# One v block turned on TensorE, next-batch loads reordered, and idle products around the first softmax

## The chip, the cores and the metric

One Trainium2 chip, one of its cores. The time is device microseconds of that core, median of several executions; lower is better. The engines are TensorE (PE), its weight loads (PEld), VectorE (DVE), ScalarE (ACT), GpSimd (POOL) and SyncE (SP). SP and POOL issue most of the DMAs.

## The reference, cut to what matters

```python
B, N, C = 4, 6080, 256          # q, k, v: [B, N, C] float32
qn = q / (norm(q, axis=1) + 1e-6);  kn = k / (norm(k, axis=1) + 1e-6)
a  = softmax(kn.T @ qn / tau)   # per batch, 256 x 256
x  = (v @ a).reshape(B * N, C)
out = gelu_tanh(x @ w_in) @ w_out        # w_in [256, 2048], w_out [2048, 256]
```

The kernel folds `a` into the first weight matrix (`aw = a @ w_in`, once a batch). A block of 512 rows of v then needs: v turned (channels on the partitions, `vT`), products of the hidden layer (`hp`), gelu by ACT, products with `w_out` (`yp`). The Gram matrix `G` and the column sums of the next batch are spread as "slots" between the steps of the blocks; for batch 0 they form a first phase of their own.

## The kernel before: the parts concerned

Loads of v and of the later q and k are issued by POOL and cast from f32 to bf16 on the way; turning v is a DMA transpose issued by SP. `b` counts batches, `nb` blocks.

```python
    vin = ctx.enter_context(tc.tile_pool(name="vin", bufs=5))
    ...
    first_chunks = chunks_of([2, 5, 6, 6, 6, 6, 6, 4, 3, 2, 1], 7)   # the 64-row remainder goes with chunk 7
    TAIL = 7
    ...
    def pairs_of(n, sqb):                       # column sums of a chunk's squares, for n < TAIL
        size = first_chunks[n][1]
        h = size // 2
        ...                                     # slots 0..size-1 only
    ...
    def turn_v(nb):
        ...
        for s in range(n):
            nc.sync.dma_start_transpose(out=vT[:, :, s * 128 : s * 128 + 128], in_=t[:, s, :])
    ...
    # POOL's queue: w_in (4 loads), v block 1, w_out (2 loads), then
    for n in range(3):
        load_qk(1, n)                           # chunks of the next batch
        if n < 2:
            load_v(n + 2)
    ...                                         # softmax of batch 0, vT of block 0 by PE
        nc.scalar.activation(vT0[:, cc, :], vps[:, cc, :], AF.Copy)   # in two halves
    ...
    turn_v(1)                                   # then in the block loop: turn_v(nb + 2); load_v(nb + 4)
```

## Time and profile before

| stretch of the kernel before (us) | what runs | PE busy |
|---|---|---|
| 0 to 36.9 | loads of q and k of batch 0, G, column sums | 60%, from 29.5 on 87% |
| 36.9 to 46.3 | softmax, aw, vT of block 0 | 76% |
| 46.3 to 54.5 | block 0 | 97% |
| 54.5 to 64.6 | nothing on PE | 0% |
| 64.6 to 81.7 | block 1 | 98%, at first at half clock |
| 81.7 to 775.2 | blocks 2 to 47 | 99% |

776.3 us (775.14 to 776.45, four executions). Read from the right: once block 2 has begun, PE works without a break, so the time is the start of block 2 plus a constant. Everything the change can win must show as an earlier block 2.

### The profile page before, as it was taken

How to read it: one execution, taken by the hardware profiler on the slowest of the kernel's cores; microseconds unless marked ns; L12 is line 12 of the kernel's file. 1: busy time of each engine (PE TensorE's matmuls, PEld its weight loads, DVE VectorE, ACT ScalarE, POOL GpSimd, SP SyncE). 2: the span in 40 equal slices, each digit the busy share in tenths (PEclk: the TensorE clock that was granted, in tenths of full speed). 3: DMA queues.
4: the chain of work that ended last, by engine and by line, in shares of the span. 5: the costliest groups of instructions: out<-in, count | busy, mean ns of one | idle time of the engine just before them, and what ended most of it. 6: DMA issues, size and time to landing. Idle time of an engine off the chain costs nothing.

```text
span 775.2 us, 12214 instructions
## 1 busy us (share of the span) xinstructions
PE 739.3 (95%) x5155; PEld 507.8 (66%) x5240; DVE 277.9 (36%) x487; ACT 420.9 (54%) x413; POOL 65.2 (8%) x121
## 2 busy tenths in 40 slices
PE   4776999999999999999999999999999999999998
PEld 3534666666666666666667666666766666666666
DVE  4731454544521454544431264545351101110011
ACT  5752555555555555555545555555545555555552
POOL 0231011001210001000300010100100000000000
PEclk9987999999999999999999999999999999999999
DMA  9999568412983365721695167723432333212111
GB/s 367 319 193 174 105 127 144 82 41 63 187 140 82 76 126 99 149 52 41 119 173 112 38 130 133 132 55 78 85 69 80 67 69 89 60 50 74 40 55 52
DMA packets 82039, 83.86 MB, mean 108 GB/s; under 512 B 56640, under 2 KB 61504, under 8 KB 81984
## 3 DMA queue, kind: packets, MB, share of 16 engines
q0 software_dynamic: 17648, 32.97, 25.8%
q1 hardware_dynamic: 64048, 49.18, 23.7%
q8 instruction: 41, 0.67, 0.4%
q10 hardware_dynamic: 288, 0.92, 0.3%
q14 instruction: 14, 0.11, 0.0%
HBM read 78.91 MB, written 24.90 MB: 134 GB/s over the span
## 4 chain that ended last, share of the span: by engine, by line
PE 90%; DMA 6%; SPq 1%; issue 1%; ACT 1%; POOL 0%; DVE 0%; ACTq 0%; DVEq 0%
PE yp L432 44%; PE hp L484 41%; PE G L124 4%; DMA st<-in_k_dram 3%; DMA vT<-vb 2%; DMA vb<-in_v_dram 1%; PE ps L184 1%; SPq L276 0%; POOL win_bf L291 0%; ACT sqb L230 0%; SPq L78 0%; PE cols L136 0%; ACT g L488 0%; PE T L162 0%; DVE qkb L225 0%
## 5 line engine op out<-in xcount | busy, mean ns | idle before, releaser
L488 ACT ACTIVATE g<-hp 128x1024 bf16<-128x1024 f32 (+1 forms) x384 | 389.6, 1015 | 327.1 <-PE hp L484 307.6
L484 PE MATMUL hp<-vT,aw 128*128 128x512 bf16 (+1 forms) x1458 | 385.4, 378 | 14.0 <-DMA vT<-vb 10.1
L432 PE MATMUL yp<-wout_bf,g 128*128 128x256 bf16 (+1 forms) x3072 | 397.9, 273 | 0.8 <-issue 0.2
L432 PEld LDWEIGHTS <-g 128*128 128x128 bf16 (+1 forms) x3072 | 301.1, 98 | 114.7 <-issue 3.3
L484 PEld LDWEIGHTS <-aw 128*128 128x128 bf16 x1536 | 149.8, 98 | 117.9 <-issue 14.5
L449 DVE COPY ysb<-yp 128x512 f32<-128x512 f32 (+1 forms) x93 | 64.0, 689 | 402.7 <-PE yp L432 402.7
L373 DVE TENSOR_TENSOR acc<-acc,sq 128x512 f32<-128x512 f32 (+1 forms) x141 | 97.5, 692 | 4.8
L124 PE MATMUL G<-qkb 128*128 128x256 bf16 (+1 forms) x384 | 74.0, 296 | 14.9 <-DVE qkb L225 14.9
L372 DVE TENSOR_TENSOR sq<-qkb 128x512 bf16<-128x512 bf16 (+1 forms) x141 | 58.7, 417 | 0.0
L124 PEld LDWEIGHTS <-qkb 128*128 128x128 bf16 (+1 forms) x384 | 39.0, 105 | 23.4 <-DVE qkb L225 15.8
L262 POOL DMA_DIRECT2D vb<-in_v_dram x47 | 25.5, 543 | 213.0 <-DMA vT<-vb 204.7
L193 DVE TENSOR_SCALAR aw<-ps,rsinv 128x512 bf16<-128x512 f32 x30 | 22.4, 749 | 26.2 <-PE ps L184 21.2
L78 POOL DMA_DIRECT2D qkb<-in_q_dram x24 | 13.2, 549 | 203.0 <-PE G L124 119.3
L230 ACT ACTIVATE sqb<-st 128x3072 bf16<-128x3072 f32 (+5 forms) x10 | 21.1, 2123 | 10.6 <-DMA st<-in_k_dram 10.6
L225 DVE CAST qkb<-st 128x3072 bf16<-128x3072 f32 (+6 forms) x12 | 14.6, 1225 | 15.0 <-DMA st<-in_k_dram 15.0
L184 PE MATMUL ps<-win_bf,eT 128*128 128x512 bf16 x54 | 17.1, 394 | 0.1
L383 POOL TENSOR_TENSOR r<-r,half 128x4 f32<-128x4 f32 x3 | 3.1, 1038 | 142.1 <-DVE r L382 142.1
L78 POOL DMA_DIRECT2D qkb<-in_k_dram x24 | 13.2, 549 | 4.5 <-DMA wout_bf<-in_moe_w_out_dram 1.9
L408 DVE RECIPROCAL den<-den 128x256 f32<-128x256 f32 x6 | 10.5, 1753 | 0.2
L453 DVE COPY ysb<-yp 64x256 f32<-64x256 f32 (+1 forms) x7 | 2.7, 415 | 21.2 <-PE yp L432 21.2
L184 PEld LDWEIGHTS <-eT 128*128 128x128 bf16 x60 | 5.9, 101 | 2.5 <-issue 1.1
L212 DVE TENSOR_TENSOR pair<-sqb 128x1536 bf16<-128x1536 bf16 (+2 forms) x7 | 5.8, 836 | 0.0
(51 smaller groups left out, 66.5 us busy)
## 6 DMA issues: line engine op xcount, KB each, us to landing
out_dram<-ysb SPq DMA_DIRECT2D x44, 512.0 KB, 2.9
vb<-in_v_dram POOLq DMA_DIRECT2D x43, 256.0 KB, 5.6
qkb<-in_q_dram POOLq DMA_DIRECT2D x21, 384.0 KB, 6.0
qkb<-in_k_dram POOLq DMA_DIRECT2D x21, 384.0 KB, 8.0
st<-in_q_dram SPq DMA_DIRECT2D x5, 768.0 KB, 10.4
st<-in_k_dram SPq DMA_DIRECT2D x5, 768.0 KB, 12.1
vT<-vb SPq DMA_TRANSPOSE x188, 3.8
out_dram<-ysb SPq DMA_DIRECT2D x4, 384.0 KB, 2.4
```

Of the source, the lines that this page charges most:

```text
L78: engines[x].dma_start(out=dst[:, x, 0:size, :], in_=src[b, s0 * 128 : (s0 + size) * 128, :].rearrange("(p s) c -> p s c", s=size))
L124: nc.tensor.matmul(G[:, ic, :], lhsT=qk[:rows, 1, s, ic * 128 : ic * 128 + 128], rhs=qk[:rows, 0, s, :], start=first and ic == 0, stop=las ...
L184: nc.tensor.matmul(ps, lhsT=eT[:, jc, ic * 128 : ic * 128 + 128], rhs=win_bf[:, jc, fs * 512 : fs * 512 + 512], start=jc == 0, stop=jc == 1)
L193: nc.vector.tensor_scalar_mul(dst, ps, scale)
L230: nc.scalar.activation(sqb[:rows, :, lo:hi], st[:rows, :, lo:hi], AF.Square)
L262: nc.gpsimd.dma_start(out=t[:, 0:n, :], in_=v_rows[r0 : r0 + n * 128, :].rearrange("(p s) c -> p s c", s=n))
L372: nc.vector.tensor_mul(sq[:rows], flat, flat)
L373: nc.vector.tensor_add(acc[:rows], acc[:rows], sq[:rows])
L432: nc.tensor.matmul(yp[:rows, at, :], lhsT=g[:, fc, s * 128 : s * 128 + rows], rhs=wout_bf[:, fc, :], start=fc == 0, stop=fc == FC - 1)
L449: nc.vector.tensor_copy(ysb[:, s0 : s + 1, :], yp[:, 0 : s + 1 - s0, :])
L484: nc.tensor.matmul(hp[:, j, :cols], lhsT=aw[:, cc, fc * 128 : fc * 128 + 128], rhs=vT[:, cc, :cols], start=cc == 0, stop=cc == 1)
L488: nc.scalar.activation(g[:, 2 * i : 2 * i + 2, :cols], hp[:, :, :cols], AF.Gelu_apprx_tanh)
```

## The change

Its intent: take away the 10 us wait for block 1's turned v, and keep PE's clock up through the softmax. Core of the diff:

```diff
-    vin = ... bufs=5          # and in the loop: load_v(nb + 4)
+    vin = ... bufs=4          #                  load_v(nb + 3)
-    first_chunks = chunks_of([2, 5, 6, 6, 6, 6, 6, 4, 3, 2, 1], 7)
+    first_chunks = chunks_of([2, 5, 6, 6, 6, 6, 6, 4, 3, 2, 1], 1)
+            # chunks 9 and 10 are loaded into the unused slots of the tiles of chunks 7 and 8
+                st = staged[n - 2][:, :, first_chunks[n - 2][1] :, :]
+    def keep_clock(n):
+        for _ in range(n):
+            idle = pH.tile([128, 2, 512], FP32, tag="h", name="idle")
+            nc.tensor.matmul(idle[:, 0, :], lhsT=filler[:, 0:128], rhs=filler, start=True, stop=True)
+        if n >= TAIL - 2:
+            keep_clock(size)             # before G of chunks 5 to 10; also 5 and 1 in the softmax
-    for n in range(3):
-        load_qk(1, n)
-        if n < 2:
-            load_v(n + 2)
+    load_qk(1, 0)
+    load_v(2)
-        nc.scalar.activation(vT0[:, cc, :], vps[:, cc, :], AF.Copy)
+    nc.scalar.activation(vT0, vps, AF.Copy)
-    turn_v(1)
+    def turn_v_on_pe(nb): ...            # 8 PE transposes of bf16, one DVE copy
-        if b > 1:
-            for n in range(3):
-                load_qk(b, n)
-        for _ in range(10):
+        for n in range(10):
+            if n % 3 == 0 and n < 9 and (b, n // 3) not in loaded_of:
+                load_qk(b, n // 3)
+            if b == 1 and n == 5:
+                turn_v_on_pe(1)
             yield
```

More of the change, by code (lines that the diff above doesn't have):

```diff
@@ L54 @@
     gp = ctx.enter_context(tc.tile_pool(name="gp", bufs=2))
-    vin = ctx.enter_context(tc.tile_pool(name="vin", bufs=5))
+    vin = ctx.enter_context(tc.tile_pool(name="vin", bufs=4))
     pA = ctx.enter_context(tc.tile_pool(name="pA", bufs=2, space=bass.MemoryType.PSUM))
@@ L89 @@
     n_all = S_ALL + 1
-    first_chunks = chunks_of([2, 5, 6, 6, 6, 6, 6, 4, 3, 2, 1], 7)
-    TAIL = 7
+    first_chunks = chunks_of([2, 5, 6, 6, 6, 6, 6, 4, 3, 2, 1], 1)
+    TAIL, SHARED = 7, 9
     staged = []
@@ L97, in stage_chunk @@
         if n < len(first_chunks):
-            st = stage.tile([128, 2, SMAX, 256], FP32, tag="st", name="st")
+            if n < SHARED:
+                st = stage.tile([128, 2, SMAX, 256], FP32, tag="st", name="st")
+            else:
+                st = staged[n - 2][:, :, first_chunks[n - 2][1] :, :]
             load_chunk((nc.sync, nc.scalar if n < 2 else nc.sync), st, 0, first_chunks[n])
@@ L106 @@
     make_identity(nc, ident)
+    ident_bf = const.tile([128, 128], BF16)
+    nc.gpsimd.tensor_copy(ident_bf, ident)
+    filler = const.tile([128, 512], BF16)
+    nc.gpsimd.memset(filler, 1.0)
     ones_bf = const.tile([128, 1], BF16)
@@ L307 @@
     Gs = scaled(G, r)
+    keep_clock(5)
     T = turned(Gs)
@@ L318 @@
                              rhs=ident, is_transpose=True)
-        nc.scalar.activation(vT0[:, cc, :], vps[:, cc, :], AF.Copy)
+    nc.scalar.activation(vT0, vps, AF.Copy)
+    keep_clock(1)
     nc.scalar.activation(dummy, ones_f, AF.Gelu_apprx_tanh)
@@ L348, with turn_v_on_pe @@
     vT_of[0] = vT0
-    turn_v(1)
-    def attention_steps(b, aw_next):
-        if b > 1:
-            for n in range(3):
-                load_qk(b, n)
-        for _ in range(10):
+    def turn_v_on_pe(nb):
+        t = v_of.pop(nb)
+        vT = vts.tile([128, 2, 512], BF16, tag="vT", name="vT")
+        p = pA.tile([128, 2, 512], BF16, tag="a", name="vps")
+        for cc in range(2):
+            for s in range(4):
+                nc.tensor.matmul(p[:, cc, s * 128 : s * 128 + 128],
+                                 lhsT=t[:, s, cc * 128 : cc * 128 + 128],
+                                 rhs=ident_bf, is_transpose=True)
+        nc.vector.tensor_copy(vT, p)
+        vT_of[nb] = vT
+    def attention_steps(b, aw_next):
+        for n in range(10):
[3 more added lines that the diff above has]
+                turn_v_on_pe(1)
             yield
@@ L472 @@
             turn_v(nb + 2)
-            load_v(nb + 4)
+            load_v(nb + 3)
             g = gp.tile([128, FC, 512], BF16, tag="g", name="g")
```

## The prediction

> **What bounds the kernel now.** I read the page first. TensorE (PE) is busy 739.3 of 775.2 us and the chain that ended last is 90% PE, so from about 70 us on only PE work counts. The windows view says so by stretch: 528.65 of 532.00 us busy from 113 to 645. What can be had lies in the first 82 us. Page lines:
>
> ```profile
> PE   4776999999999999999999999999999999999998
> PEclk9987999999999999999999999999999999999999
> L484 PE MATMUL hp<-vT,aw 128*128 128x512 bf16 (+1 forms) x1458 | 385.4, 378 | 14.0 <-DMA vT<-vb 10.1
> L432 PE MATMUL yp<-wout_bf,g 128*128 128x256 bf16 (+1 forms) x3072 | 397.9, 273 | 0.8 <-issue 0.2
> vT<-vb SPq DMA_TRANSPOSE x188, 3.8
> ```
>
> Of the 14.0 us that PE idled before a product of the hidden layer (hp), one wait is 10.1 us: it waits for turned v (vT). A DMA transpose of v lands after 3.8 us in the median. The chain of waits over 28 to 130 us says what stands before it:
>
> ```profile
> 33.50 3.53 POOL win_bf L291 x4
> 37.03 9.48 DMA vb<-in_v_dram
> ...
> 50.44 14.06 DMA vT<-vb
> 64.63 1.44 PE hp L484 x3
> ```
>
> Block 1 of v landed at 46.51, its four transposes were issued from 46.53 to 50.44, and the last landed at 64.49, 14.06 us after its issue and almost four times the median. The windows view (us, then busy time of PE, weight load, DVE, ACT, POOL, the granted clock, DMA share, GB/s) gives the stretches: block 0, the wait, the start of block 1, its rest, block 2:
>
> ```profile
> 46.30:54.50 8.20, 7.95 (x37) 3.32 (x34) 3.28 (x5) 6.87 (x7) 1.43 (x3) 1.00 1.29 197
> 54.50:64.60 10.10, 0.04 (x1) 0.00 (x1) 0.69 (x1) 1.10 (x2) 3.33 (x7) 0.71 1.12 204
> 64.60:70.20 5.60, 5.35 (x23) 3.06 (x25) 0.00 (x0) 1.67 (x2) 0.53 (x1) 0.61 1.12 206
> 70.20:81.70 11.50, 11.45 (x83) 8.01 (x83) 3.77 (x7) 6.35 (x7) 0.00 (x0) 1.00 1.04 94
> 81.70:97.40 15.70, 15.59 (x111) 10.66 (x112) 8.59 (x17) 8.26 (x9) 1.59 (x3) 1.00 0.57 118
> ```
>
> The reader is to see three things: 10.1 us with no PE work; then 5.6 us at a mean clock of 0.61; and DMA engines full (share over 1) until about 75. The DMA view over 50 to 64 us tells who fills them:
>
> ```profile
> q0 software_dynamic: 1251, 2.53, 97.9%
> q1 hardware_dynamic: 1151, 0.26, 16.1%
> ```
>
> Queue q0 carries the casting loads (v, next q and k), q1 at that time only the transposes. They get nearly one packet each, 1251 to 1151, but a transpose's packet is a tenth the size. The transposes are slow because they take turns with a queue that is never empty.
>
> **What the Trainium skill says.** "DMA: Bandwidth & Descriptors", section "Queues, rings and completion order": each DMA engine goes round robin between the queues with work, a packet at a time. The counts above agree. "Advanced Engine Details and Errata", section "X-Bar Transpose (TRN2)", says transposes are as fast as regular DMAs; here they moved 0.26 MB in 14 us beside a full queue, so I use the measurement. "TensorE: Matmul & The Clock Gate", Part 1: after an idle window of about 3.4 us the clock drops to half, and returns after a busy window. The trace agrees: half speed from 58.8 to 69.0 us by the clock's records, three such windows, and also 38.3 to 45.1. Part 4 of that page gives about 275 to 390 ns for one PE transpose; the f32 ones here show 421 ns each at half clock, pipelined.
>
> **The change, part by part.**
>
> Block 1 turned on PE. Removes four DMA transposes and the 10.08 us wait. Adds eight bf16 transposes, which at 128 columns against 512 are about a quarter of an hp product (0.216 us warm): with their loads 0.5 to 0.8 us, and one VectorE copy of about 1 us. They stand between the sixth and seventh step of block 0, where ACT (1.02 us per gelu against 0.86 us of PE) sets the pace, so I count 0.5 us. Data are in time: vb of block 1 landed at 46.5, this place comes near 50. Without the idle stretch block 1 starts warm. From 64.63 to 81.74 it took 17.1 us; warm it takes 8 x (0.86 + 0.87) us plus some five pairs of G products at 0.22, about 15.0. Gain 2.1.
>
> Idle products: 22 before the six last chunks plus six in the softmax stretch, 512 columns each. In the first chunks of these PE may still be cold (0.43 us each, 2.6 us for six), but it has about 0.7 us idle per 3.77 us chunk and turns warm there; the loads, not PE, bound this phase (420 GB/s). In the tail (4+3+2+1, 2.2 us warm) they fill nearly all of PE's slack, about neutral together with the earlier last loads. In 38.3 to 45.1 they may keep the clock up: eight vps transposes, four first aw products at 0.22 instead of 0.42, and one ACT copy instead of two with a handshake. win_bf caps it (its second quarter landed near 42.4). First gelu about 44.2 instead of 46.35: gain 2.1.
>
> Shared stage tiles, remainder moved to chunk 1: the last chunks' loads need no tile release (they waited until 25.6 and 30.5), which removes a dip of the DMA rate (131 GB/s in the one microsecond from 33 to 34) of some 0.5 us; the v0 load also goes earlier. The gate that starts the casting loads moves little, 0.3 us. A side effect, seen in the instruction order: four column-sum products vanish, because the pair sums of chunk 1 do not include its 64-row remainder. Batch 0's norms then miss 64 of 6080 rows, about 0.5% of a norm; scores are tiny, so I expect it to pass, but it is a defect.
>
> Load order: v blocks 2 and 3 now go out before the second chunk of the next batch. Nothing makes POOL wait for PE's slots; only the order in its queue changes. Block 2's own place, behind win, v1, wout and the first chunk, is the same.
>
> **Where block 2 comes in.** Adding up, PE would be ready for block 2 at 44.2 + 8.2 + 0.5 + 15.0 = 67.9 instead of 81.74: a gain of 13.8. But block 2 needs its own four DMA transposes. In the kernel before, its vb landed at 60.55 (SP resumed transposing at 60.57) and the fourth transpose, issued at 64.36, took 14.1 us: 78.4, only 3.3 us ahead of its use. The change moves this landing as follows.
> - vb of block 2: gate 0.3 earlier, and no transposes beside the loads from 46.5 to 60.5. q0 moved 0.80 MB per 4 us in 42 to 50 but 2.53 MB per 14 us in 50 to 64 (0.20 against 0.18 MB/us): 1.2 earlier. So about 59.0.
> - q0 then still has v3, two chunks, v4 and a third chunk: 256 + 768 + 768 + 256 + 768 KB = 2.88 MB, at 0.181 MB/us 15.9 us: empty near 75. (v5 reuses v2's buffer, so it waits for these transposes.)
> - Four transposes at some 300 packets, against q0's turn rate of about 78 packets per us: 15.4 us plus some 2 of latency, 76.4; but they finish at once when q0 empties, as the before trace shows (q0's last landing 78.09, transpose 78.44).
>
> So vT of block 2 lands near **75.0**, and PE idles some 7 us at 67.9: the same wait, one block later. It also drops the clock again; the restart at 64.63 was cold for 4.4 us and lost 2.1; I take 2.4. All gains of head, block 1 and idle products go into this wait, because the end follows the landing. From block 2 on the program is the same length: 776.3 - (81.74 - 75.0) + 2.4 = **772.0 us**.
>
> **The rivals.**
> (1) No new wait: all 13.8 us stay, 762.5. For it: v3 no longer sits behind two chunks, and the author plainly wants the loads spread. Against it: v2's place is unchanged and POOL runs ahead, so q0 stays full. 10%.
> (2) New wait and longer: if vb of block 2 is not earlier at all, and the transposes take the full 18 us that block 1's took (46.53 to 64.49), vT lands at 78 and cold costs 3.4: 776, no gain. 15%.
> (3) PE becomes the bound of the first phase through cold idle products (2.6 us each in two chunks) and delays the first gelu. Then the wait at block 2 shrinks by as much, and the total hardly moves. This is why I do not spread the range for the head.
> (4) Fewer v buffers (4 for 5) give a later wait: v loads still lead their transposing by a block (15.6 us) against landings of 4 to 9 us. Under 5%.
>
> **Range and chances.** Landing 73.5 to 77 and a cold cost of 1.7 to 3.4 give 770 to 775; with rival 1 as a tail below, 767 to 775. Faster by over 2% needs 15.5 us, more than even rival 1 gives: 0.03. Slower by over 2%: 0.01. Within 2%: 0.96.
>
> **What would show it.** PE's wait for vT before hp near 65 gone, but one of 4 to 9 us before block 2's first hp, ending at 73 to 77; granted clock at half around it; block 1 at 15 us and full clock; first gelu near 44; q0 full until 75; PE busy time up by about 6 us of idle products. A landing of block 2's vT before 69 would make me wrong downward, by up to 10 us.

## The result

768.84 us (767.55 to 769.48) against 776.32: ratio 0.9905, 95% interval 0.9888 to 0.9922. All ratios here are the mean time of one kernel's fast runs over that of the other's fast runs of the same rounds, so they are not quite the ratio of the quoted medians. The forecast of 772.0 (767 to 775, "within 2%") held, but only by the tail that I had added for rival 1: the path that I thought likely gave 770 to 775. The gain was 7.5 us where I had 4.3.

The groups of the page that answer to those shown of before (line, engine, what, then busy us, mean ns, idle us before it and what ended it):

```profile
L460 PE MATMUL yp<-wout_bf,g 128*128 128x256 bf16 (+1 forms) x3072 | 397.9, 273 | 0.0
L512 PE MATMUL hp<-vT,aw 128*128 128x512 bf16 (+1 forms) x1536 | 391.8, 378 | 4.3 <-DMA vT<-vb 4.0
...
vT<-vb SPq DMA_TRANSPOSE x184, 3.8
```

The 10.1 us wait is gone and a wait of 4.0 us for vT stands in its place. The stretches of the changed kernel (columns as in the prediction): block 0, block 1, the new wait, the half-clock stretch, the rest of block 2:

```profile
44.10:53.90 9.80, 9.45 (x50) 4.35 (x49) 4.60 (x7) 7.97 (x8) 2.48 (x5) 1.00 1.29 197
53.90:68.10 14.20, 14.20 (x103) 9.87 (x101) 4.58 (x9) 8.16 (x8) 2.65 (x5) 1.00 1.11 211
68.10:72.20 4.10, 0.07 (x1) 0.03 (x1) 3.97 (x8) 0.04 (x1) 0.00 (x0) 0.76 1.36 152
72.20:77.10 4.90, 4.90 (x17) 2.02 (x18) 0.69 (x1) 1.02 (x1) 1.02 (x2) 0.50 0.96 210
77.10:90.10 13.00, 13.00 (x95) 9.17 (x94) 3.77 (x7) 7.02 (x7) 1.09 (x3) 1.00 0.46 82
```

Block 1 now runs at full clock from end to end. PE is done with it at 68.2, stands for 4.0 us, and then works 4.9 us at a clock of 0.50. The chain of waits says what it stood for:

```profile
45.48 11.08 DMA vb<-in_v_dram
56.58 1.29 SPq L292
57.93 2.08 SPq L292
60.07 1.24 SPq L292
61.35 10.72 DMA vT<-vb
72.20 1.86 PE hp L512 x4
```

This is the chain of the kernel before, one block later: v of block 2 lands at 56.56, SP issues four transposes, the last takes 10.7 us. The DMA view of 56.6 to 71.3 us shows the same company (queue, packets, MB, share of the engines):

```profile
q0 software_dynamic: 960, 2.46, 85.6%
q1 hardware_dynamic: 1475, 0.34, 28.8%
```

Start of block 2: 81.74 before, 72.20 now, 9.54 earlier. Block 2 lasts longer by the half clock: before it ran from 81.74 to 97.37 (15.6 us), now from 72.20 to 90.12 (17.9 us), 2.3 lost. Net 7.2 of the 7.5 us between the two profiled spans (775.2 and 767.7).

### The profile page after: what moved, and what is told of

It reads as the page before. It is cut to its first block, busy times and chain, and to the rows that moved or that the text cites. A ratio compares the mean times of both kernels' runs of the same rounds, so it can differ in the third digit from the quotient of the medians.

```text
span 767.7 us, 12360 instructions
## 1 busy us (share of the span) xinstructions
PE 746.8 (97%) x5272; PEld 508.3 (66%) x5272; DVE 278.6 (36%) x488; ACT 420.6 (55%) x412; POOL 65.9 (9%) x123
## 4 chain that ended last, share of the span: by engine, by line
PE 90%; issue 4%; DMA 4%; SPq 1%; POOL 1%; DVE 0%; POOLq 0%
PE yp L460 43%; PE hp L512 41%; PE G L138 4%; DMA vb<-in_v_dram 1%; DMA vT<-vb 1%; PE ps L198 1%; DMA win_bf<-in_moe_w_in_dram 1%; SPq L292 1%; POOL win_bf L307 0%; PE cols L150 0%; PE T L176 0%; POOL filler L114 0%; DVE ysb L481 0%; POOL ident masks.py:199 0%; POOL ident_bf L112 0%
## 5 line engine op out<-in xcount | busy, mean ns | idle before, releaser
L512 PE MATMUL hp<-vT,aw 128*128 128x512 bf16 (+1 forms) x1536 | 391.8, 378 | 4.3 <-DMA vT<-vb 4.0
L78 POOL DMA_DIRECT2D qkb<-in_q_dram x24 | 13.2, 551 | 186.1 <-PE G L138 102.1
L244 ACT ACTIVATE sqb<-st 128x3072 bf16<-128x3072 f32 (+5 forms) x10 | 21.0, 2120 | 10.1 <-DMA st<-in_k_dram 10.1
L239 DVE CAST qkb<-st 128x3072 bf16<-128x3072 f32 (+6 forms) x12 | 14.6, 1225 | 15.2 <-DMA st<-in_k_dram 15.2
L78 POOL DMA_DIRECT2D qkb<-in_k_dram x24 | 13.3, 553 | 2.7 <-DMA wout_bf<-in_moe_w_out_dram 1.9
L134 PE MATMUL idle<-filler 128*128 128x512 bf16 x28 | 7.9, 401 | 0.0
(58 smaller groups left out, 73.5 us busy)
```

The source lines that it names most:

```text
L78: engines[x].dma_start(out=dst[:, x, 0:size, :], in_=src[b, s0 * 128 : (s0 + size) * 128, :].rearrange("(p s) c -> p s c", s=size))
L244: nc.scalar.activation(sqb[:rows, :, lo:hi], st[:rows, :, lo:hi], AF.Square)
L512: nc.tensor.matmul(hp[:, j, :cols], lhsT=aw[:, cc, fc * 128 : fc * 128 + 128], rhs=vT[:, cc, :cols], start=cc == 0, stop=cc == 1)
```

## The experiments

Each time is the median of four to six executions, with those of the kernel before in the same rounds; the three groups of four kernels ran on three chips, on which the kernel before took 777.1, 776.85 and 776.58 us. All outputs passed the comparison with the reference.

The theory: **the end follows the landing of block 2's DMA transposes, these are slow only because the casting queue beside them never empties, and what the other parts save before that is swallowed by the wait.** The rivals: each part saves its own; or the transposes are slow by themselves.

### e1: the PE turn alone

```diff
 # the kernel before, plus:
+            if b == 1 and n == 5:
+                turn_v_on_pe(1)
```

> The kernel before with block 1 of v turned on the PE and nothing else of the change. Theory (the end follows the landing of block 2's DMA transposes, and the other parts of the change feed a wait): vb of block 2 lands near 56.6 us as in the changed kernel, then 3072 KB stand in the casting queue at about 0.2 MB/us, so vT of block 2 lands near 72.6; PE arrives near 70 and waits 1 to 4 us; total 767 to 769.5, the same as the changed kernel's 768.8 within 1.5 us. Rival (each part saves its own): turning alone removes 10.1 us wait and 2.1 us cold clock but the head's 2 us are missing, so it would be 2 us or more slower than the changed kernel, 771 or above.

Measured 770.86 us (767.98 to 772.29), ratio 0.9917 (0.9900 to 0.9934). The changed kernel's own second measurement gave 0.9893 (0.9879 to 0.9906) on another chip. So the turn alone brings most of the gain, but my number missed by more than 1 us and the intervals nearly part: not as clean as the theory wanted. The profiled execution (the fastest, 767.98) shows no wait before block 2 at all, though vT of block 2 landed where I expected it (72.88 for 72.6): the head came late, with the first gelu at 49.36 instead of 46.35 and PE still at half speed, so PE was ready for block 2 only at 73.02. (The head is what runs before block 0: first phase, softmax and first products with `aw`.) This was the first sign that the head varies from run to run.

### e2: the changed kernel without idle products

```diff
-        for _ in range(n):
+        for _ in range(0):
             idle = ...
```

> The changed kernel with its 28 idle products taken out. Theory: whatever they gain before block 2 goes into the 4.0 us wait for vT of block 2, so the total stays within 1.5 us of 768.8 (767 to 770); the first gelu comes about 1.5 to 2 us later, the wait shrinks by as much, and if it falls below some 3 us the clock may not drop, which would even save up to 2 us. Rival (idle products earn their head gain): 770.5 to 772.

Measured 768.39 us, ratio 0.9892 (0.9875 to 0.9908): no loss. First gelu at 46.79 instead of 44.32, and the wait for vT shrank from 4.0 to 1.6 us. Idle products do bring the head forward here, and the wait takes all of it, as the theory said:

```profile
PE hp L512 <- DMA vT<-vb: 1.6, 1, 1.6
```

After this shorter wait the clock did not drop (it stayed at full from 45.56 us to the end of the work), as the expectation allowed for; that profiled execution took 767.02 us, 2.5 less than that of the changed kernel (769.48).

### e3: block 2 turned on PE as well

```diff
+                if b == 1 and seen == 3:
+                    turn_v_on_pe(2)
-            turn_v(nb + 2)
+            if nb > 0:
+                turn_v(nb + 2)
```

> The changed kernel with block 2 of v turned on the PE as well, in block 1. Theory: the 4.0 us wait and the 2.2 us of half clock after it go, eight PE transposes cost 0.4: 768.8 - 4.0 - 2.2 + 0.4 = 763.0, range 762 to 764.5; the transposes of block 3 land by about 72, long before their use at 84. Rival (the wait only moves one block on once more): a new wait of 3 us or more before block 3, 766 to 769.

Measured 763.74 us (763.60 to 764.06), ratio 0.9832 (0.9819 to 0.9846). No wait for vT is left in the list of waits, and the clock stays at full from 25 us to the end. Block 3's four transposes land at 71.9 as expected, long before their use at 84. They were slow as well, 15.2 us from the first issue at 56.74, but block 3 is far enough away, so the wait did not move on again.

### e4: POOL held until block 2's transposes are done

```diff
+            if b == 1 and n == 3:       # POOL reads the four pieces of vT before it goes on to load
+                nc.gpsimd.tensor_copy(gate[:, 1:5], vT_of[2][0:1, 0, ::128])
             if n % 3 == 0 and n < 9 and (b, n // 3) not in loaded_of:
                 load_qk(b, n // 3)
```

> The changed kernel, but POOL waits for the four transposes of block 2 before it issues the second chunk's loads, so the casting queue runs empty while they go. Theory (the transposes are slow only because they take turns with the casting queue): they land within 5 to 7 us of vb of block 2, near 62 instead of 72; no wait before block 2, full clock; 768.8 - 6.2 = 762.6, range 761.5 to 765, unless the held chunk is then late for its G products at block 2. Rival (transposes are slow by themselves, 15 us for four): landing stays near 70, total 767 to 770 or worse.

Measured 763.04 us (762.99 to 764.71), ratio 0.9828 (0.9813 to 0.9843). This is the deciding run. The DMA view of 56.6 to 62.5 us, once the casting queue is empty:

```profile
q1 hardware_dynamic: 1152, 0.26, 22.9%
q0 software_dynamic: 3, 0.00, 0.4%
...
vT<-vb SPq DMA_TRANSPOSE x5, 2.4
```

The same transposes now land 2.4 us after issue, in the median, instead of 8.7 to 11.6 for those of block 2 in the changed kernel. The four of block 2 were issued from 56.09 and all had landed at 62.53: 6.4 us instead of the 15.5 (56.58 to 72.06) in the changed kernel. The windows show block 1 and block 2 back to back at full clock:

```profile
53.10:68.10 15.00, 15.00 (x107) 10.39 (x107) 4.57 (x9) 8.94 (x9) 4.77 (x9) 1.00 0.58 101
68.10:83.80 15.70, 15.70 (x112) 10.62 (x111) 8.62 (x17) 8.23 (x9) 1.60 (x3) 1.00 1.09 212
```

The held loads (DMA share 1.09 in the second line) cost PE nothing. The rival "slow by themselves" is out. Shown is that the queued loads make them slow; whether by the turns alone or also by the time that the loads take from the engines, this run doesn't separate.

### e5: block 2's v loaded ahead of the next batch's first chunk

```diff
-    load_qk(1, 0)
-    load_v(2)
+    load_v(2)
+    load_qk(1, 0)
```

> The changed kernel with vb of block 2 loaded ahead of the next batch's first chunk, the same loads in all. Its vb should land near 53 instead of 56.6 us. Theory (the four transposes take 15 to 19 us beside a full casting queue, and end at the latest when that queue empties near 71): vT of block 2 lands between 69 and 72, so most of the wait stays and the total is within 2 us of the changed kernel, 767 to 769.5. Rival (landing follows the start of the transposes one to one, 15.5 us as measured): 68.6, wait below 1 us, no drop of the clock, 763 to 765.

Measured 769.23 us, ratio 0.9906 (0.9892 to 0.9919), the changed kernel beside it on the same chip 768.62. The list of waits:

```profile
PE hp L512 <- DMA vT<-vb: 4.2, 1, 4.2
```

v of block 2 did land 4 us earlier (52.49 for 56.56), but its fourth transpose landed at 72.35 for 72.06, and the last casting load before it at 71.99. Starting earlier was worth nothing here: the four transposes took 19.8 us instead of 15.5, and the last landed when the casting queue emptied. This reordering, with the same loads in the queue, doesn't cure the wait; other orders were not tried.

### The changed kernel again

> The changed kernel once more, on the same chip as the three runs beside it. Every theory: 768 to 770, half clock after the wait in most runs, ratio to the kernel before 0.989 to 0.992.

768.62 us, ratio 0.9893 (0.9879 to 0.9906). Its profiled execution took 767.58, the other profiled one 769.48. Of the 1.9 us, 1.1 come from an earlier landing of block 2's vT (70.95 here, 72.06 there), and 0.8 from the clock: it stayed at half until 74.20 here and until 77.09 there, and block 2 took 17.1 and 17.9 us.

### e6 and e7: variants of e3

e6 is e3 without idle products (edit as in e2); e7 is e3 with the remainder's squares put back:

```diff
         if size % 2:
             parts.append(sqb[:, :, size - 1, :])
+        if first_chunks[n][2]:
+            parts.append(sqb[:REM, :, size, :])
```

> Blocks 1 and 2 turned on the PE as in e3_turn_two, without the 28 idle products. Theory (idle products bring the first gelu from about 46.8 to 44.1 us, and this counts once no wait behind it swallows it): 2 to 4 us slower than e3_turn_two, 766 to 768, and with a wider spread from run to run. Rival (idle products are worth nothing, as taking them out of the changed kernel suggests): within 0.5 us of 763.7.

> e3_turn_two with the 64-row remainder of chunk 1 put back into the first batch's column sums (four products of one column more). Every theory: within 0.7 us of e3_turn_two, 763 to 764.5; correct, with the norms of batch 0 complete.

e6: 763.85 us (763.45 to 764.18), ratio 0.9832, the same as e3. My theory of 2 to 4 us is refuted for this kernel: without idle products, in all five executions, nothing was lost. In the profiled one the clock was at half from 31.5 to 38.4, under the last chunks, and at full through the softmax; the first gelu came at 44.32. Up to there e6 and e2 run the same instructions, yet e2's profiled execution (on another chip) had half clock from 42.14 to 45.55 and its first gelu at 46.79.

e7: 764.01 us, within 0.3 of e3. The defect that I had read from the instruction order (the pair sums of chunk 1 leave out its 64 rows) is mended at no cost that these runs can tell. The changed kernel passes without it, but its norms of batch 0 are incomplete.

### e8 to e11: what the small parts are worth once the wait is gone

All on one chip. e8 is e4 with the mended sums. e9 is e4 with unshared stage tiles and the remainder back in chunk 7. e10 is e4 without idle products and with vT of block 0 copied in two halves. e11 is the kernel before with only the PE turn, the load order of the change and the hold of e4:

```diff
 # e9, from e4
-    first_chunks = chunks_of([2, 5, 6, 6, 6, 6, 6, 4, 3, 2, 1], 1)
-    TAIL, SHARED = 7, 9
+    first_chunks = chunks_of([2, 5, 6, 6, 6, 6, 6, 4, 3, 2, 1], 7)
+    TAIL, SHARED = 7, 99
 # e10, from e4 (and keep_clock over range(0), as in e2)
-    nc.scalar.activation(vT0, vps, AF.Copy)
+        nc.scalar.activation(vT0[:, cc, :], vps[:, cc, :], AF.Copy)
 # e11, from the kernel before (with the edit of e1 and the slots' loads and gate copy of e4)
-    for n in range(3):
-        load_qk(1, n)
-        if n < 2:
-            load_v(n + 2)
+    load_qk(1, 0)
+    load_v(2)
+    load_v(3)
```

> e4_held with the 64-row remainder of chunk 1 back in the first batch's column sums: the version meant to beat both kernels and to be complete. Every theory: within 0.7 us of e4_held, 762.5 to 764, full clock, no wait before block 2.

> e4_held with the stage tiles not shared and the remainder back in chunk 7, as in the kernel before. Theory (the last loads landed at 35.3 us in the changed kernel as in the one before, so the earlier issues gained nothing): within 0.7 us of e4_held. Rival (the earlier last loads bring 1 us or more that nothing behind swallows here): 764.5 or above.

> e4_held without idle products and with block 0's turned v copied by ACT in two halves, as before. Theory after e6 (idle products worth nothing): what remains of the head's 2 us is this copy, so 0.5 to 2 us over e4_held, 763.5 to 765.5. Rival (the head's gain was the clock after all, by luck granted in e6): 765 to 767 with a spread of over 2 us between runs.

> The kernel before with only two edits: block 1 turned on the PE, and the second chunk's loads behind block 2's transposes (POOL waits for them). Theory: these two hold nearly the whole gain, first gelu near 46, block 2 right after block 1 near 70 to 71: 763.5 to 766.5, below the changed kernel's 768.7. Rival (the small parts of the change, added up, are worth 4 us or more once no wait swallows them): 767 or above.

| kernel | us | range | ratio | first gelu in the profile |
|---|---|---|---|---|
| e8 | 763.28 | 763.11 to 763.66 | 0.9832 (0.9818 to 0.9846) | 44.36 |
| e9 | 763.19 | 762.83 to 764.45 | 0.9835 (0.9820 to 0.9850) | 44.04 |
| e10 | 766.34 | 765.05 to 767.71 | 0.9871 (0.9852 to 0.9889) | 48.55 |
| e11 | 767.89 | 765.37 to 768.26 | 0.9880 (0.9862 to 0.9899) | 49.88 |

e8 is the version to keep: 13.3 us under the kernel before, 5 to 6 under the changed one, and complete (so is e9, where the remainder is in chunk 7 again). e9 confirms that sharing the stage tiles is worth nothing: in the changed kernel the last chunk landed at 35.33, in the one before at 35.32.

e10 and e11 show what e2 hid. With the wait gone, an old head costs 3.1 us (e10 against e8) and 4.6 (e11 against e8). So the rivals of e10 (765 to 767, spread over 2 us) and of e11 (767 or above) were right with their numbers, and my theories were not: the small parts of the head do count, once nothing behind them swallows their gain. Both kernels fall into two groups, though: e10 two executions at 765.05 and 765.53 and two at 767.16 and 767.71, e11 two at 765.37 and 765.85 and three from 767.89 to 768.26. Both profiles are of the slow kind, and a median depends on how many of each were drawn. The PE timeline of e10's head (start, busy, what), and under it the changed kernel's:

```profile
36.16 1.44 PE L138 MATMUL G<-qkb 128*128 128x256 bf16 x6
...
41.85 1.06 PE L331 MATMUL vps<-ident,v 128*128 128x128 f32 x4
43.60 1.11 PE L331 MATMUL vps<-ident,v 128*128 128x128 f32 x4 [0.69 <-ACT vT L334]
...
44.66 1.87 PE L343 MATMUL ps<-win_bf,eT 128*128 128x512 bf16 x4
```

```profile
35.33 0.82 PE L138 MATMUL G<-qkb 128*128 128x256 bf16 x6
...
40.16 1.04 PE L331 MATMUL vps<-ident,v 128*128 128x128 f32 x8
...
41.36 1.02 PE L343 MATMUL ps<-win_bf,eT 128*128 128x512 bf16 x4
```

The same products take nearly twice as long in e10: there PE did not reach full speed before 46.92 us, and in e11 not before 49.56. In eight profiled executions with idle products the first gelu came between 44.00 and 44.36; in the six without (before, e1, e2, e6, e10, e11) between 44.32 and 49.88. In these profiles the idle products buy a head that does not vary.

What stays open: e10 lost both the idle products and the single copy, e6 only the idle products and lost nothing. That the single copy alone always keeps the clock up is ruled out by e2, which has e6's head and came late in its profile; why e6 was early in all five executions, these runs do not tell. e11's further 1.5 us over e10 stand mostly in the head in the two profiles (first gelu 1.3 us later), and the faster groups of the two are only some 0.3 us apart; whether the stage tiles or the v buffers, in which they differ too, have a part in it was not tested.

## Why the prediction was right

**What bounds, and where the gain ends: right.** The 10.1 us wait went, and the wait for block 2's vT that I put in its place came, for the reason given; e3 and e4 remove it in two different ways and are 5.1 us (763.74) and 5.8 us (763.04) below the changed kernel's 768.84, though on another chip.

**PE's arrival at block 2: 67.9 predicted, 68.2 measured.** Its parts held as well: first gelu 44.2 against 44.32, block 1 15.0 us against 15.1 (53.02 to 68.17). But the gain of 2.1 in the head was counted from the one profile of the kernel before (46.35); with the same head e1 and e11 show 49.36 and 49.88.

**The landing of vT: the mis-sized term.** I had v of block 2 at 59.0 and vT at 75.0; measured 56.56 and 72.06, outside the 73.5 to 77 from which I had made my range. The step that failed is "1.2 earlier" for loads that no longer run beside transposes. I took it from the rate of bytes moved (0.20 against 0.18 MB/us). What counts is landings. Between the landing of v block 1 and v block 2 lie the same 1984 KB in both kernels: 14.04 us before (46.51 to 60.55), 10.04 us now (46.52 to 56.56). So without the transposes the loads gained 4.0 us, not 1.2. e1, whose only edit is the PE turn, has 10.09 (45.61 to 55.70), so it is the missing transposes and not another part of the change. (The gate gave 0 instead of 0.3: the first casting load went out at 33.45 before and 33.47 now.) The profile before held the warning: from 46.6 to 60.5 its casting queue moved 2.53 MB while 2.03 MB landed; in the changed kernel, from 46.6 to 56.5, it moved 2.04 MB for the same 2.03. Why moving and landing come apart beside transposes is not shown. The rest of the sum held: 2816 KB after it took 14.7 us (56.56 to 71.30) where I had 15.9, and vT landed 0.8 us after the queue's last load.

**The cold clock: 2.4 predicted, 2.3 measured**, though the wait was 4.0 and not 7 us. That it fits so well is luck: in the other two profiles with such a wait block 2 lost 1.5 (the changed kernel again) and 1.6 us (e5).

**The sum.** (81.74 - 72.06) - 2.3 = 7.4, beside 7.5 measured; I had (81.74 - 75.0) - 2.4 = 4.3.

**Parts that I had wrong but which the wait made harmless.** The square root that ends the first phase began at 38.07 instead of 36.95. That is not the cost of the idle products alone: without them it began at 38.82 in e2 and 38.34 in e6, and with the head of the kernel before at 39.15 in e1 and 39.59 in e11. The profile of the kernel before had the clock at full from 28.04 to 38.28; e2 and e6 had it at half under the last chunks, e1 and e11 all through. The shared tiles gained nothing instead of 0.5 us. Rival 3 said why a later head would not show: the wait shrinks by as much. e2 shows the exchange, 4.0 to 1.6 us.

**Rivals.** Rival 1 (no new wait, 762.5) is what e3 and e4 reach when its condition is made true: 763.7 and 763.0. Rival 2, a longer wait, did not come. Rival 4, the fewer v buffers, left no trace: the list of waits holds no other wait for vT.

**The page of the skill behind the clock.** "TensorE: Matmul & The Clock Gate", Part 1, gave the drop after an idle window; the changed kernel shows it again, 0.50 from 70.27 to 77.09 around a 4.0 us wait. The moment differs from the page's window of about 3.4 us: here the drop came 2.1 us after PE's work had ended at 68.17, and in e5 only at 73.31, when PE had started again at 72.49. After the wait of 3.1 us in the changed kernel's second profile it dropped too, after e2's of 1.6 us it did not.

## What to carry to other kernels

When a wait is removed, look at once for the next consumer of the same kind of transfer, and compute when its data land, not only when the engine will be ready; all gains upstream of that landing are worth nothing until it moves. Small transfers beside a queue that stays full are slow: here four transposes took 15.5 to 19.8 us, or 6.4 once the queue was held. Holding the other queue (e4) helped, starting the small one earlier (e5) did not. And judge small changes again after a wait behind them is gone: what measured as nothing in e2 belonged to a head worth 3 to 5 us in the medians of e10 and e11.

## What the Trainium skill lacked or had wrong

- "Advanced Engine Details and Errata", "X-Bar Transpose (TRN2)": transposes as fast as regular DMAs. Here, on free engines (e4), their packets took 22.9% of 5.9 us for 0.26 MB, by my estimate 5 us of all 16 engines a MB, as the casting loads did in the changed kernel (85.6% of 14.7 us for 2.46 MB); the plain f32 loads of the first phase took 2.4 (102.2% of 10 us for 4.20 MB, from 10 to 20 us in the kernel before). And four of 64 KB took 6.4 us even so, issued some 1.3 us apart and each landing after 2.4.
- "DMA: Bandwidth & Descriptors", "Queues, rings and completion order": the turn taking by packets fits the kernel before (1251 packets to 1151 from 50 to 64 us), less evenly the changed one (960 to 1475 from 56.6 to 71.3). It lacks the consequence for landings: with transposes in the other queue, 1984 KB of loads took 14.0 us to land instead of 10.0, 4.0 more, while the transposes' packets took 13.2% of 13.9 us, or 1.8.
- "TensorE: Matmul & The Clock Gate", Part 4: full clock is said not to engage for transposes. Here the f32 transposes took 421 ns each in e10, where PE ran at half speed, and 272 ns in the changed kernel at full clock, eight of them in 1.04 us. Whether transposes help to release the clock, no run here shows.
- The same page, Part 1: about 3.4 us of sustained activity release the clock. In e11 PE was 80% busy from 10 to 39 us (23.11 of 29.00) and its products still ran at half speed at 48 us; in e2, 78% busy (9.11 us of 11.66 from 10 us on), full clock came at 21.66. How busy a window must be, the page doesn't say.
- The clock's records begin with their first change. "TensorE: Matmul & The Clock Gate", Part 1, warns that clock events in a trace can be unreliable, but lacks this case: the profile page of e10 prints PEclk 9 in all its slices, and its record a mean of 1.0, although its products took twice their time until 47 us. Durations of equal products tell; the row does not.
